# Soft-capped attention with a top-1 expert layer: earlier value loads, ScalarE's releases without GpSimd, a last tile of 32 rows in column tiles

## Chip, cores and metric

One core of a Trainium2 chip runs the whole kernel in one launch. The metric is the device time of one execution in microseconds (us); the median of several executions is compared. Engines are named as in the profile: PE is TensorE (matmul), PEld its weight load, DVE VectorE, ACT ScalarE, POOL GpSimd, SP SyncE.

## What is computed

```python
def _attn_ref(q, k, v, cap):                   # 4 batches, 12 heads, 448 rows, 64 columns
    scores = matmul(q, k.T) / sqrt(64)
    scores = cap * tanh(scores / cap)
    attn = softmax(scores)
    return matmul(attn, v)

def _moe_ref(x, expert_emb, tau, w1, w2):      # x: 1792 x 768, 8 experts, F = 1024
    logits = normed(x) @ normed(expert_emb).T / tau
    e = argmax(logits); gate = softmax(logits)[e]
    out[row] = gate * (relu(x[row] @ w1[e]) @ w2[e])
```

The attention's output, with its heads side by side, is the expert layer's `x`. Each row goes to one expert. With these inputs the experts get 592, 513, 403, 150, 129, 5, 0 and 0 rows, in the order in which the kernel takes them.

## The kernel before

**Attention.** The 48 heads are taken in 24 pairs, two pairs to a unit; a unit has 7 steps. A step makes scores on PE, `tanh` and `exp` on ACT (L860, L864) and, some steps later, the value product on PE (L899), whose rows carry 64 values, 8 columns of the values times the experts' embeddings and a column of ones for the denominator. The embedding columns are made by PE and copied by DVE (L881) into the loaded value rows `vb`. DVE also splits queries and keys into a high and a low part (L828, L829), divides by the denominator and does the routing's counting. `load_heads` (L398 and on) loads keys and queries `qkb`, values `vb` and transposed values `vt` by SP, each into a ring of 2 or 3 buffers. `PARTS` (L74) says at which step of a unit which of the three is loaded, and how many units behind. `odd_heads` (L933) shifts half a batch's columns by a DMA on the same SP queue once DVE has written them, and L463 and L467 write x to a table in DRAM, `x_dram`.

**Expert layer.** All products are in f16 with high and low parts, three matmuls for one. Weights come by SP (`w1r`, `w2r`), and ACT (high part, L250) and DVE (low part, L251) split and scale them for the next expert while PE works on this one. GpSimd fetches 128 rows of x at a time by indirect DMA (`gather`, L221), scales them (`scale_x`, L227), PE turns them round (L238), and ACT and DVE split them into `xh` and `xl` (L241, L242). `tile_body` is a full tile of 128 rows: `up` (L260, 144 matmuls), relu into `hh` and `hl` (L272, L273), and downs (L700) into two PSUM banks, `held`. The output stays there: `release`, at the start of the next tile, scales it on ACT by `held_g` (L311), and GpSimd scatters it to the output rows `held_i` (L312). Up to 32 rows that an expert has beyond its full tiles ride along with one tile of it: `wide_tile` has 160 columns in up (L1475), and the 32 rows' down product is the *along product* (L1518): `hidden` of 32 rows as the stationary side and four column tiles of 32 columns of PE's array, each for a quarter of the 768 output columns. Its output `yo_a` goes through ACT (L1526) and GpSimd (L1527). Here the first expert has five full tiles (the first, hidden under the end of attention, two, and `more0_1`, `more0_2`), the second to fifth have wide tiles (p = 1 to 4) and full ones as needed, and the sixth a half tile (p = 5, 64 columns).

Each tile is inside a branch on a count. At the end of a branch each engine has an exit block (L1607 for the wide tiles, L1646 at the end); GpSimd's waits for all DMAs that it started and then updates their semaphores.

`pace` (FIRST, FIRST0, L86) gives the number of weight splits before each half of up and before each down step. `hooks` run small work at given steps. Instructions go to each engine's queue in program order. The slot of `yo` in `release` comes from two buffers that full tiles share (`tile_of("o")`).

## Time and profile before

| | |
|---|---|
| Time, median of 3 runs (lowest to highest) | 483.21 us (481.74 to 484.41) |
| The profiled execution's own time | 484.38 us |
| Its span in the profile | 482.7 us |
| PE busy | 439.6 us (91%) |
| ACT, DVE, POOL busy | 275.0, 259.9, 126.5 us |
| Mean granted clock of PE | 0.966 |

The span runs from the first instruction to the last, with 1.7 us of the execution outside. Attention and the routing fill it to about 203 us, the expert layer the rest. Times in the text are us from the span's start; in a row of a timeline the number in brackets is how long the engine was idle before the instruction, and what ended that.

### The profile page before, as it was taken

The page shows a single profiled execution, that of the slowest core. Times are in us where ns is not written, and L with a number is a line of the kernel's source. Part 1 is how long each engine was busy: PE and PEld are TensorE (multiplying, and loading weights), DVE is VectorE, ACT ScalarE, POOL GpSimd, SP SyncE. Part 2 cuts the span into 40 slices and gives each one's busy share as a digit, 9 for nine tenths or more (in the row PEclk, how much of TensorE's full clock was granted, in tenths as well). Part 3 has the DMA queues.
Part 4 walks back from the last instruction along what each step waited for, and adds up shares of the span by engine and source line. Part 5 has one row for each costly group of instructions (what it writes and reads, how often), then busy time and mean ns, then how long its engine had stood idle before and what let it go on. Part 6 is the DMA issues. An engine that isn't in the chain of part 4 may idle for free. (4 is left out here: it accounts for less than half of the span.)

```text
span 482.7 us, 16495 instructions
## 1 busy us (share of the span) xinstructions
PE 439.6 (91%) x7001; PEld 352.7 (73%) x7002; DVE 259.9 (54%) x679; ACT 275.0 (57%) x308; POOL 126.5 (26%) x230
## 2 busy tenths in 40 slices
PE   7999998998999699998789989999999999997771
PEld 3788886877878689677477877887887886875561
DVE  5254466558969699884651159211159111964910
ACT  3999998796999786533642067122076122836610
POOL 5000000000010212124362164332155332563720
PEclk9899999898999989999899999999999999998977
DMA  6824559544678652055980269620258521891020
GB/s 194 305 59 143 205 174 336 184 138 177 200 245 255 188 201 88 6 177 186 378 329 3 71 245 406 266 71 1 72 155 309 210 71 19 285 317 56 5 54 27
DMA packets 32457, 82.22 MB, mean 170 GB/s; under 512 B 8253, under 2 KB 13337, under 8 KB 32354
## 3 DMA queue, kind: packets, MB, share of 16 engines
q1 hardware_dynamic: 28754, 67.35, 40.5%
q0 software_dynamic: 2816, 13.49, 8.6%
q8 instruction: 62, 1.02, 0.8%
q14 instruction: 41, 0.34, 0.2%
q10 hardware_dynamic: 784, 0.03, 0.1%
HBM read 68.81 MB, written 12.31 MB: 168 GB/s over the span
## 5 line engine op out<-in xcount | busy, mean ns | idle before, releaser
L899 PEld LDWEIGHTS v<-vb,prob 128*64 128x64 f32 (+1 forms) x2688 | 83.6, 142 | 16.0 <-issue 15.0
L860 ACT ACTIVATE prob<-s,icap 128x896 f32<-128x896 f32 x84 | 80.5, 999 | 18.9 <-PE s L850 15.8
L899 PE MATMUL v<-vb,prob 128*64 128x73 f32 (+1 forms) x2688 | 90.7, 235 | 0.0
L260 PEld LDWEIGHTS <-h 128*128 128x128 f16 x1056 | 79.7, 99 | 5.5 <-issue 3.0
L260 PE MATMUL h<-xh,h 128*128 128x128 f16 (+1 forms) x480 | 78.8, 219 | 3.7 <-DVEq L1607 2.6
L260 PE MATMUL h<-xl,h 128*128 128x128 f16 (+1 forms) x480 | 78.7, 219 | 0.3
L260 PE MATMUL h<-xh,l 128*128 128x128 f16 (+1 forms) x480 | 78.7, 219 | 0.0
L864 ACT ACTIVATE prob<-prob,cap_b 128x1792 f32<-128x1792 f32 (+1 forms) x47 | 76.7, 1632 | 1.5
L251 DVE SCALAR_TENSOR_TENSOR l<-w1r,by_pos,h 128x1024 f16<-128x1024 f32 x30 | 37.1, 1282 | 31.6 <-ACT h L250 31.6
L700 PEld LDWEIGHTS <-hh 128*128 128x128 f16 (+1 forms) x352 | 33.2, 102 | 27.0 <-ACT hh L272 5.7
L260 PEld LDWEIGHTS <-l 128*128 128x128 f16 x528 | 52.1, 99 | 0.5 <-issue 0.5
L700 PE MATMUL v<-h,hh 128*128 128x384 f16 (+1 forms) x176 | 43.0, 338 | 6.3 <-ACT hh L272 5.4
L273 DVE SCALAR_TENSOR_TENSOR hl<-h,hh 128x512 f16<-128x512 f32 (+1 forms) x20 | 13.1, 663 | 65.7 <-ACT hh L272 65.7
L227 POOL TENSOR_TENSOR x_tile<-xg 128x768 f32<-128x768 f32 x16 | 28.4, 1775 | 70.3 <-PE xt L238 65.9
L1475 PE MATMUL h<-xh,h 128*128 128x160 f16 x192 | 39.9, 233 | 3.5 <-PEq L1607 1.4
L700 PE MATMUL v<-l,hh 128*128 128x384 f16 (+1 forms) x176 | 43.0, 337 | 0.0
L700 PE MATMUL v<-h,hl 128*128 128x384 f16 (+1 forms) x176 | 42.6, 335 | 0.0
L251 DVE SCALAR_TENSOR_TENSOR l<-w2r,by_pos,h 128x1536 f16<-128x1536 f32 x20 | 40.4, 2055 | 3.7 <-ACT h L250 3.7
L272 ACT ACTIVATE hh<-h 128x512 f16<-128x512 f32 (+1 forms) x20 | 11.4, 574 | 50.2 <-PE h L260 28.3
L1475 PE MATMUL h<-xh,l 128*128 128x160 f16 x192 | 39.9, 233 | 0.0
L1475 PE MATMUL h<-xl,h 128*128 128x160 f16 x192 | 39.9, 233 | 0.0
L241 ACT CAST xh<-xt 128x384 f16<-128x384 f32 x30 | 12.8, 478 | 45.2 <-PE xt L238 45.2
(287 smaller groups left out, 797.1 us busy)
## 6 DMA issues: line engine op xcount, KB each, us to landing
w1r<-in_moe_w_dram SPq DMA_DIRECT2D x30, 512.0 KB, 9.1
w2r<-in_moe_w_dram SPq DMA_DIRECT2D x20, 768.0 KB, 7.0
qkb<-in_qk_pairs_dram SPq DMA_DIRECT2D x11, 896.0 KB, 6.8
vb<-in_v_pairs_dram SPq DMA_DIRECT2D x12, 511.0 KB, 5.2
vt<-in_vt_pairs_dram SPq DMA_DIRECT2D x12, 448.0 KB, 7.1
x_dram<-xsb SPq DMA_DIRECT2D x12, 432.0 KB, 3.9
ring<-in_moe_w_dram SPq DMA_DIRECT2D x6, 512.0 KB, 5.6
ring<-in_moe_w_dram SPq DMA_DIRECT2D x5, 384.0 KB, 4.5
```

The lines of the kernel that those rows point to most:

```text
L227: nc.gpsimd.tensor_tensor(x_tile.rearrange("p (h d) -> p h d", d=DH), heads(xg[:, :SCALE]), xg[:, SCALE : SCALE + 1].unsqueeze(2).to_broad ...
L241: nc.scalar.copy(hi, t)
L251: nc.vector.scalar_tensor_tensor(out=lo, in0=raw, scalar=scale, in1=hi, op0=ALU.mult, op1=ALU.subtract, accum_out=acc)
L260: nc.tensor.matmul(hp[:, f, :W], l[j][:, c], x[:, j, :W], start=j == 0 and f == 0 and n == 0, stop=j == DC - 1 and f == 3 and n == 2, skip ...
L272: nc.scalar.activation(b, a, AF.Relu)
L273: nc.vector.scalar_tensor_tensor(out=c, in0=a, scalar=0.0, in1=b, op0=ALU.max, op1=ALU.subtract, accum_out=acc[:, h : h + 1])
L700: nc.tensor.matmul(y, hidden[h][l][:, c, :W], w2p[p % 2][w][f // 2][:, f % 2, m * C : (m + 1) * C], start=f == 0 and n == 0, stop=f == FC ...
L860: nc.scalar.activation(o, sp[:, :, :S], AF.Tanh, scale=icap)
L864: nc.scalar.activation(o, o, AF.Exp, scale=cap_b)
L899: nc.tensor.matmul(psum_v[2 * i + n][h * DH : (h + 1) * DH, m * VW : (m + 1) * VW], pt[rows, s, c : c + DH], vb[rows, k, s, :], start=m == ...
L1475: nc.tensor.matmul(o, w1p[p % 2][l][j][:, c], x[:, j, :], start=j == 0 and f == fs[0] and m == 0, stop=j == DC - 1 and f == fs[-1] and m == 2,
```

## The change

1. The value rows are loaded in the sixth step of a unit instead of in the second of the next, the transposed values and the keys a step or several earlier (`PARTS`).
2. The order of small work around the first tiles: `token_rows` of the last batch moves from before the first tile's downs to the second tile's start; the routing's last pieces move into the ups; `FIRST0` puts one weight split instead of three and two before the first two halves of chain 0's first tile; the along rows' transposes use PSUM banks of their own.
3. `gate` and `held_g` are computed by ACT instead of GpSimd. Releases in wide tiles and in the last tile write to `rows[p % 2]`, two slots of their own in `room`.
4. In `wide_tile` the along product stands before the transposes of the next x, and its output in ACT's and GpSimd's queues with it; the last wide tile leaves `scale_x` and `gather` to the branch for further tiles.
5. The sixth and later experts' last rows, now up to 32 instead of 64, go through `small_tile`: x is the stationary side (32 columns), the weights move through four column tiles, then the hidden layer is turned round by two transposes.

```diff
-PARTS = {5: ("k", 0), 0: ("t", 1), 2: ("v", 1)}
+PARTS = {2: ("t", 0), 4: ("k", 0), 6: ("v", 0)}
-FIRST, FIRST0 = (4, 4, 1), (3, 2, 1)
+FIRST, FIRST0 = (4, 4, 1), (1, 1, 1)
 ...
-    def hold(idx, unscaled):
-        nc.gpsimd.tensor_tensor(held_g, gate, unscaled, op=ALU.mult)
+    def hold_rows(idx):
         nc.gpsimd.tensor_copy(held_i, idx)
-    def release():
-        yo = tile_of("o", 0)
+    def hold_gates(unscaled):
+        nc.scalar.activation(held_g, gate, AF.Copy, scale=unscaled)
+    def release(yo=None):
+        yo = tile_of("o", 0) if yo is None else yo
 ...
     def wide_tile(...)
-        release()
+        release(rows[p % 2])
 ...
+        hold_gates(unscaled)
+        hold_rows(col(base))
 ...
-        transpose_x()
-        scale_x()
-        ya = tile_of("h", 0)
+        ya = tile_of("s", 0)
         for f in range(FC):
             ...
-        down(6)
-        down(7)
         nc.scalar.activation(yo, ya[:, :C], AF.Copy, scale=ga)
         nc.gpsimd.indirect_dma_start(out=..., in_=yo, ...)
-        gather(col(base + 3))
+        transpose_x()
+        if p + 1 < WIDE.stop:
+            scale_x()
+        down(6)
+        down(7)
+        if p + 1 < WIDE.stop:
+            gather(col(base + 3))
 ...
+    def small_tile(p, before=()):
+        ...
+        for m in range(BLOCKS):
+            nc.scalar.activation(
+                gt[m * TAIL : (m + 1) * TAIL], gate[:TAIL], AF.Copy, scale=by_pos[:TAIL, 2, p : p + 1]
+            )
+        for j in range(DC):
+            for k, (x, w) in enumerate(((xh, 0), (xl, 0), (xh, 1))):
+                for m in range(BLOCKS):
+                    nc.tensor.matmul(
+                        hp[m * TAIL : (m + 1) * TAIL], x[:, j, :TAIL], w1p[p % 2][w][j][:, m * n : (m + 1) * n], ...
+                    )
+        nc.scalar.copy(h32, hp)
+        for c in range(2):
+            nc.tensor.transpose(t[:, c * P : (c + 1) * P], h32[:, c * P : (c + 1) * P], ident)
+        relu(0, t[:, : 2 * P].rearrange("p (c t) -> p c t", t=P), acc, (hh, hl))
+        for f in range(FC):
+            for k, (l, w) in enumerate(passes):
+                for m in range(BLOCKS):
+                    nc.tensor.matmul(
+                        y[m * TAIL : (m + 1) * TAIL], (hh, hl)[l][:, f % 2, b],
+                        w2p[p % 2][w][f // 2][:, f % 2, m * C : (m + 1) * C], ...
+                    )
+        nc.vector.tensor_scalar(yo, y, gt, None, op0=ALU.mult)
+        nc.gpsimd.indirect_dma_start(out=..., in_=yo, ...)
 ...
-            half_tile(p, {0: [lambda: foretell("more", ends[p][0] > 1), release]}, fine_sums)
+            small_tile(p, [lambda: release(rows[p % 2])])
+            foretell("more", ends[p][0] > 1)
+            fine_sums()
             overflow(False)
```

**SP in attention.** `vb` are value rows, `qkb` keys and queries, `vt` transposed values; the copies of `xsb` on itself are `odd_heads`. Before, around the first late load of value rows:

```order
28 L933 DMA xsb_201<-xsb_201 64x2x72
29 L463 DMA x_dram<-xsb_201 384x1x288
30 L403 DMA qkb_207<-in_qk_pairs_dram 128x2x896
31 L467 DMA x_dram<-xsb_201 64x864
32 L403 DMA vt_212<-in_vt_pairs_dram 128x896
33 L933 DMA xsb_202<-xsb_202 64x2x72
34 L463 DMA x_dram<-xsb_202 384x1x288
35 L403 DMA vb_210<-in_v_pairs_dram 128x1022
```

With the change, from the same `odd_heads` copy on:

```order
29 L908 DMA xsb_198<-xsb_198 64x2x72
30 L464 DMA x_dram<-xsb_198 384x1x288
31 L404 DMA qkb_204<-in_qk_pairs_dram 128x2x896
32 L404 DMA vb_207<-in_v_pairs_dram 128x1022
33 L468 DMA x_dram<-xsb_198 64x864
34 L908 DMA xsb_199<-xsb_199 64x2x72
```

The value rows of the unit (`vb_210` before, `vb_207` now) moved from behind the second `odd_heads` copy to right behind the unit's `qkb`.

**ACT at the end of the last wide tile** (`w2r` are raw weights, `yo_a` the along product's output, `held_g` the output's scale). Before:

```order
381 L250 ACTIVATE h_4836<-w2r_4850,by_pos 128x1536
382 L250 ACTIVATE h_4837<-w2r_4851,by_pos 128x1536
383 L250 ACTIVATE h_4838<-w2r_4852,by_pos 128x1536
384 L241 CAST xh<-xt_8439 128x3x128
385 L241 CAST xh<-xt_8445 128x3x128
386 L1526 ACTIVATE yo_a<-h_8454,gta 128x192
387 L1607 COMPARE_AND_BRANCH
```

With the change:

```order
410 L249 ACTIVATE h_4825<-w2r_4839,by_pos 128x1536
411 L249 ACTIVATE h_4826<-w2r_4840,by_pos 128x1536
412 L249 ACTIVATE h_4827<-w2r_4841,by_pos 128x1536
413 L1489 ACTIVATE yo_a<-s_8444,gta 128x192
414 L240 CAST xh<-xt_8546 128x3x128
415 L240 CAST xh<-xt_8552 128x3x128
416 L242 COPY gates_179<-gates_179 128x1
417 L1630 COMPARE_AND_BRANCH
```

`yo_a` moved from behind both halves of `xh` to before them, and a gate copy that was GpSimd's follows them.

**POOL at the same place.** `xg` is the gathered x, `x_tile` the scaled one. Before:

```order
505 L243 COPY gates_182<-gates_182 128x1
506 L227 TENSOR_TENSOR x_tile<-xg 128x768
507 L231 COPY gates_182<-xg 128x1
508 L1527 DMA out_dram<-yo_a,idx_a 7168x192
509 L220 ISA
510 L220 COPY idx_in<-table 128x1
511 L221 DMA xg<-x_dram,idx_in 128x866
512 L1607 COMPARE_AND_BRANCH
```

With the change (`room` now holds the released rows):

```order
474 L303 COPY held_i<-table 128x1
475 L1490 DMA out_dram<-yo_a,idx_a 7168x192
476 L1630 COMPARE_AND_BRANCH
477 L226 TENSOR_TENSOR x_tile<-xg 128x768
478 L230 COPY gates_179<-xg 128x1
479 L219 ISA
480 L219 COPY idx_in<-table 128x1
481 L220 DMA xg<-x_dram,idx_in 128x866
```

The two gate copies L243 and the scaling, L227, stood before the write of `yo_a`; now the write comes first and the branch L1630 right behind it, and scaling and gather stand in that branch's body, which is not taken here.

## Rows read from the trace of the kernel before

**Rows 1.** Busy time by stretch; core 0: us, then each engine's busy us, clock, DMA.

```profile
40.00:60.00 20.00, 20.00 (x428) 16.10 (x428) 9.20 (x18) 19.50 (x17) 0.25 (x2) 1.00 0.46 151
84.00:88.00 4.00, 3.50 (x44) 2.78 (x44) 2.69 (x7) 2.13 (x2) 1.13 (x2) 0.57 0.39 156
```

**Rows 2.** Table of waits: us in total, times, longest.

```profile
DVE vb L881 <- DMA vb<-in_v_pairs_dram: 15.9, 4, 4.1
```

**Rows 3.** Timeline of SyncE's queue: start, us, engine, line, what.

```profile
59.72 0.57 SPq L403 DMA_DIRECT2D qkb<-in_qk_pairs_dram  x1
...
70.76 0.62 SPq L933 DMA_DIRECT2D xsb<-xsb  x1
...
72.13 0.56 SPq L403 DMA_DIRECT2D vb<-in_v_pairs_dram  x1
```

**Rows 4.** The tile vb, all its loads.

```profile
DMA to landing us min/median/max: 4.9/5.2/7.2
```

**Rows 5.** Timeline of ScalarE behind three stalls; in brackets its idle time before.

```profile
85.83 1.01 ACT L860 ACTIVATE prob<-s,icap 128x896 f32<-128x896 f32 x1 [2.77 <-PE s L850]
...
89.64 1.91 ACT L860 ACTIVATE prob<-s,icap 128x896 f32<-128x896 f32 x2 [0.98 <-PE s L850]
...
111.28 1.91 ACT L860 ACTIVATE prob<-s,icap 128x896 f32<-128x896 f32 x2 [2.48 <-PE s L850]
...
116.56 1.91 ACT L860 ACTIVATE prob<-s,icap 128x896 f32<-128x896 f32 x2 [1.55 <-PE s L856]
...
169.91 1.97 ACT L860 ACTIVATE prob<-s,icap 128x896 f32<-128x896 f32 x2 [3.71 <-PE s L850]
...
174.98 1.91 ACT L860 ACTIVATE prob<-s,icap 128x896 f32<-128x896 f32 x2 [1.27 <-PE s L856]
```

**Rows 6.** Timeline of TensorE, ScalarE and VectorE in chain 0's first tile.

```profile
234.87 0.82 PE L700 MATMUL v<-h,hh 128*128 128x384 f16 x2 [2.82 <-ACT hh L272]
...
242.98 1.57 ACT L250 ACTIVATE h<-w2r,by_pos 128x1536 f16<-128x1536 f32 x1 [2.11 <-DMA w2r<-in_moe_w_dram]
...
246.34 1.02 DVE L242 TENSOR_TENSOR xl<-xt,xh 128x384 f16<-128x384 f32 x2
...
247.04 0.92 PE L1423 MATMUL along_t<-ident,room 128*128 128x128 f32 x6 [1.80 <-DVE xl L242]
```

**Rows 7.** Timeline of TensorE: first matmuls of the last tiles, and a gap.

```profile
408.23 0.23 PE L1475 MATMUL h<-xh,h 128*128 128x160 f16 x1 [0.74 <-PEq L1607]
...
426.88 0.50 PE L1501 MATMUL v<-h,hh 128*128 128x384 f16 x2
...
429.82 0.23 PE L1475 MATMUL h<-xh,h 128*128 128x160 f16 x1 [0.82 <-DVEq L1607]
...
458.91 0.19 PE L260 MATMUL h<-xh,h 128*128 128x64 f16 x1 [2.61 <-DVEq L1607]
...
467.37 0.53 PE L700 MATMUL v<-h,hh 128*64 128x384 f16 x2 [2.56 <-ACT hh L272]
```

**Rows 8.** Timeline of ScalarE and VectorE, fifth expert and half tile.

```profile
438.39 1.05 ACT L311 ACTIVATE yo<-v,held_g 128x384 f32<-128x384 f32 x2 [10.90 <-DMA out_dram<-yo,held_i]
...
466.94 0.66 ACT L272 ACTIVATE hh<-h 128x256 f16<-128x256 f32 x2
...
467.35 0.42 DVE L273 SCALAR_TENSOR_TENSOR hl<-h,hh 128x256 f16<-128x256 f32 x1 [8.65 <-ACT hh L272]
```

**Rows 9.** Instructions of line 1607, the ends of the tile branches, 427 to 445 us.

```profile
L1607 POOLq INC_SWDGE_SEM  x1: 806/806/806, 437.5 to 437.5; - x1
```

**Rows 10.** Timeline of GpSimd, fifth expert and last write.

```profile
440.24 1.02 POOL L312 DMA_INDIRECT out_dram<-yo,held_i  x1 [8.78 <-ACT yo L311]
443.54 0.72 POOL L1447 TENSOR_TENSOR gta<-along_g,by_pos 32x1 f32<-32x1 f32 x1 [2.27 <-issue]
...
448.51 0.41 POOL L1453 COPY gta<-gta 32x1 f32<-32x1 f32 x2
...
473.89 0.98 POOL L742 DMA_INDIRECT out_dram<-yo,idx_out  x1 [4.12 <-DVE redo_i L1571]
```

**Rows 11.** Busy time of line 1518, the along product, in one wide tile.

```profile
298.60:300.90 2.30, 2.17 (x96) 1.94 (x96) 1.00 1.01 388
```

**Rows 12.** The tile yo_a, its four writes.

```profile
DMA to landing us min/median/max: 5.5/6.3/6.5
```

More of the change, by code (lines that the diff above doesn't have):

```diff
@@ L144, in attention_moe @@
         nc.gpsimd.memset(round_up[:, n, :], float(P - 1 - (1 - n) * TAIL))
-    blocks_of = {}
-    for n in (2, 4):
-        blocks_of[n] = const.tile([P, 1], I32, name=f"block{n}")
-        for m in range(n):
-            nc.gpsimd.memset(blocks_of[n][m * P // n : (m + 1) * P // n], m)
+    BLOCKS = P // TAIL
+    block = const.tile([P, 1], I32, name="block")
+    for m in range(BLOCKS):
+        nc.gpsimd.memset(block[m * TAIL : (m + 1) * TAIL], m)
     tok = const.tile([P, B, 4], F32, name="tok")
@@ L242, in transpose_x @@
             nc.vector.tensor_tensor(lo, t, hi, op=ALU.subtract)
-        nc.gpsimd.tensor_copy(gate, gate_s)
+        nc.scalar.copy(gate, gate_s)
     def split(raw, hi, lo, scale, acc, vector=False):
@@ L654, in tiles, with tile_body @@
             nc.vector.tensor_tensor(done_full, done, full[:, 0, :], op=ALU.add)
-        def tile_body(p, idx, nxt, W=P, todo=(), pace=FIRST, hooks=(), hidden=None, first=False, before=None, holds=True):
+        def tile_body(p, idx, nxt, todo=(), pace=FIRST, hooks=(), hidden=None, first=False, holds=True):
             hooks, todo = dict(hooks), list(todo)
@@ L663, in tile_body @@
             if holds:
-                yb = [t[:, :384] for t in held]
                 if not first:
@@ L700, in down @@
                         nc.tensor.matmul(
-                            y, hidden[h][l][:, c, :W], w2p[p % 2][w][f // 2][:, f % 2, m * C : (m + 1) * C],
-                            start=f == 0 and n == 0, stop=f == FC - 1 and n == 2, skip_group_check=W < P,
-                        )
-            if first:
-                hold(idx, unscaled)
+                            y, hidden[h][l][:, c, :], w2p[p % 2][w][f // 2][:, f % 2, m * 384 : (m + 1) * 384],
+                            start=f == 0 and n == 0, stop=f == FC - 1 and n == 2,
+                        )
             if not hidden:
@@ L714, in tile_body @@
                         hook(h * DC + j)
-                        if holds and (h, j) == (1, 1):
-                            hold(idx, unscaled)
-                        up(w1p[p % 2], h, j, hp[h], W)
-                    hidden.append(relu(h, hp[h], acc, W))
+                        up(w1p[p % 2], h, j, hp[h])
+                    hidden.append(relu(h, hp[h], acc))
                 nc.vector.tensor_tensor(sum_h[:, :2], sum_h[:, :2], acc, op=ALU.add)
+            if holds:
+                hold_gates(unscaled)
+                hold_rows(idx)
             for f in range(6):
@@ L1058, in attention_bounded @@
                 ready = {
-                    0: [do_fill, do_fill], 3: square[:1], 5: [*square[1:], lambda: norms_x(last)],
+                    0: [lambda: [f() for _, _, f in route], do_fill, do_fill], 3: square[:1], 5: [*square[1:], lambda: norms_x(last)],
                     7: [count_last, do_fill], 8: [do_fill],
@@ L1069, in attention_bounded @@
                     do_fill()
-                for _, _, f in route:
-                    f()
-                token_rows(last)
                 tile_body(0, idx0[:, 0:1], None, hidden=first_h, first=True)
@@ L1353, in attention_moe @@
         0: [
-            lambda: scales_x(last), lambda: gates(last), lambda: gates_e(last), order, start_loads,
+            lambda: token_rows(last), lambda: scales_x(last), lambda: gates(last), lambda: gates_e(last), order, start_loads,
             lambda: gates_out(last), slots,
@@ L1546, in col @@
         return table[:, bass.ds(t, 1)]
-    def any_tile(p, slot, nxt, *args, **kw):
-        tile_body(p, col(slot), nxt is not False and col(nxt), *args, **kw)
     def full_tile(p, slot, *args, **kw):
-        any_tile(p, slot, slot + 3, P, *args, holds=p < WIDE.stop, **kw)
+        tile_body(p, col(slot), col(slot + 3), *args, holds=p < WIDE.stop, **kw)
+    rows = [room[:, n * D : (n + 1) * D] for n in range(2)]
     fine = work.tile([P, NF], F32, tag="fine", name="fine")
@@ L1590, in todo_for @@
             return [(split1, p, i) for i in range(SOON if p == 1 else 0, N1)] + [(split2, p, f) for f in range(N2)]
-        def half_tile(p, hooks=(), before=None):
-            any_tile(p, ends[p][1], False, P // 2, hooks=hooks, before=before, holds=False)
         def chain(p):
@@ L1660, in attention_moe @@
                 load2(LATE, f, True)
+            with tc.If(ends[WIDE.stop - 1][0] >> 1 == 1):
+                scale_x()
+                gather(col(ends[WIDE.stop][1] + 2))
             position(WIDE.stop)
```

119 lines of the change are left out of this document (65 added, 54 removed).

## Prediction

> **What bounds the kernel now.** I read the busy time by stretch first. In an undisturbed stretch of attention TensorE is busy 20.00 of 20.00 us at a granted clock of 1.00 and ScalarE 19.50 [rows 1]: both are full, so time lost there by either is not made up. In the stretch 84 to 88 us the clock is 0.57, the lower of its two levels (1.2 GHz) for most of it [rows 1], and it follows an empty TensorE. So I looked next, in the table of waits and the timelines, for what empties TensorE. Three places stand out: VectorE waits for the value rows `vb` in attention (15.9 us in four times) [rows 2]; the first expert tile waits for its hidden layer [rows 6]; and the end of the kernel, where ScalarE stands 10.90 us before the fifth expert's release and TensorE then waits 2.61 and 2.56 us [rows 7, 8]. What TensorE does elsewhere the change leaves alone.
>
> **A, attention: the loads.** SyncE issues the key load at 59.72 but the value rows only at 72.13, behind the odd-heads copy that waits for VectorE [rows 3]; they land about 5.2 us later [rows 4], and VectorE's copy L881 stands in front of all its other work until then. The change issues the value rows right behind the key load of the same unit, some 12 us earlier, so they lie there before the copy comes to them. On SyncE the writes of x and the weight loads go behind one more issue of 0.56 to 0.57 us [rows 3]; they are read many us later, which hides it. The stalls' worth I take from ScalarE, which was full: its idle gaps behind three of the four are 2.77 + 0.98, 2.48 + 1.55 and 3.71 + 1.27, together 12.76 us [rows 5] (the second gap of each pair is TensorE at the lower clock). The fourth left no such gap and counts nothing. 12.76 is a ceiling, since ScalarE has half a us of idle in 20 anyway [rows 1]: I take **-12.0**. Bounds: -13.5, if the lower clock cost a little beyond ScalarE's gaps, and -3, if only one stall goes and VectorE's own work is late next in the other two.
>
> **B, the first tiles.** The hidden layer of chain 0's first tile stands behind weight splits on ScalarE that wait for DMA; TensorE waits 2.82 us for it [rows 6]. With one split before each half instead of three and two, it no longer does. But the last `w2r` split waits for its load until 242.98 whatever comes before, VectorE's `xl` stands behind that split's second half until 246.34, and TensorE waits for `xl` [rows 6]. So most of the 2.82 us is a wait moved, not removed: Up of the next tile can start when the first `xl` half is there, near 246.9, while before it came behind the along rows' transposes, 0.92 us from 247.04 [rows 6]; these now have PSUM tiles of their own and go ahead of it. I take **-0.9**. The token rows, moved from before the first tile into the next one's start, and the gates' write, moved earlier, touch waits on VectorE and SyncE in front of a TensorE gap that ScalarE ends; nothing for them. Bounds 0 (the load stays the bound) and -2.8 (the whole gap goes).
>
> **C, wide tiles.** The along product (2.17 us, [rows 11]) goes before the transposes of the next x. `xh` and `xl` then have only two down steps as cover instead of these and the product, as in a full tile. On ScalarE the product's output `yo_a` now stands before `xh`; on GpSimd its write stands before the scaling of x and the gather, which come some 2 us later and are needed a tile later. I take **0**, between -1 and +3.6 (twice the 1.80 us that TensorE waits for `xl` where it is late, [rows 6]).
>
> **D, into the fifth expert's wide tile.** ScalarE's release at 438.39 had waited 10.90 us [rows 8]: it needs `held_g` from GpSimd, and GpSimd was in its exit block, whose semaphore update came at 437.5 and took 0.8, once the tile's gather and writes had landed [rows 9]. All weight splits, the hidden layer and VectorE's tail stand behind it, and so the half tile starts at 458.91 [rows 7]. After the change `held_g` and the gate are ScalarE's own, and the release writes into a slot that was read two tiles ago. ScalarE then starts with TensorE, as in the tile before, which took 429.82 - 408.23 = 21.59 us with its exit [rows 7]. The small tile would start at 429.82 + 21.59 = 451.4 instead of 458.91: -7.5. Next in line is `yo_a`, which needs `gta` from GpSimd: GpSimd still sits in its exit block to 438.3, and its chain ended at 448.9 [rows 10]. The product would end about 447.6: 451.4 less 2.94, from the first matmul behind the product, 426.88, to the next tile's [rows 7], and less 0.9 for six transposes [rows 6]. So `yo_a` waits about 1.3 us and `xh`, `xl` come at 450.2 and 450.8: still in time, with 0.6 us to spare.
>
> **E, the small tile and the end.** Up becomes 18 groups of four matmuls of 256 columns, each in a quarter of the array. The same form at 192 columns took 2.17 us for 24 groups, 90 ns each [rows 11]; by columns 120 ns, 18 x 0.12 = 2.2 us instead of 5.9 (458.91 to 464.8). Then a copy, two transposes, relu and the low half: by the evictions of 128x256 (0.33 each on ScalarE, 0.42 on VectorE, [rows 8]) and about 0.8 for the transposes and hand-overs, 1.9 us of TensorE idle instead of 2.56. Downs: 24 groups of 192 columns, 2.2 us as in rows 11 (up to 4.3 if the clock is at its lower level). Output scaling 0.4. TensorE's side is ready at 451.4 + 2.2 + 1.9 + 2.2 + 0.4 = 458.1.
>
> GpSimd's side: `yo_a` is written from 449.4; it has no gather beside it any more. Its landing took 5.5 to 6.5 us under load [rows 12]; the release's took 3.3 (440.24 to 443.54, [rows 10]) on a quiet chip. Between 3.0 and 5.5 I take 4.0, nearer the quiet row because the chip is quiet here: 453.4. Exit block 0.8 [rows 9] and branches 0.5: release issued 454.7. The final write waits for that release's landing, 3.3 on: 458.0, and 0.3 of branch and semaphore. So both sides are ready near 458 to 459, and I take 459.0 against 473.89 [rows 10]: **-14.9** for D and E, between -16 and -11.5 (landings of 5.5, and the lower clock for down). The time from this issue to the span's end, 482.7 - 473.89 = 8.8 [rows 10], stays: the sums and the test for overflow, now behind the output, take 1.7 us beside its landing.
> By the Trainium skill ("DMA: Bandwidth & Descriptors", "Anatomy of one DMA — SWDGE (gpsimd) path") a write costs about 2.0 us fixed plus its bytes at 436 GB/s: an estimate of 2.2 and 2.9 us for the two landings in place of 4.0 and 3.3. By that rule GpSimd's side would be ready 2.2 us earlier, TensorE's 458.1 would rule, and D and E would give -15.8. The rows at hand (3.3 and 5.5) lie above the rule's figures, so the sum keeps them.
>
> **Sum.** -12.0 - 0.9 + 0 - 14.9 = -27.8. On the profiled run's 484.4 that is 456.6. That run is 1.2 above the median of the runs shown, 483.2: I forecast **455.4** for a median.
>
> **Rivals.**
> 1. *The loads help little* (A fails): a load can't start before its slot in the ring is free, and VectorE may be late by itself. Against it: the slots are of three units ago, and the key loads at the same point of the queue do go out [rows 3]. Only one stall gone, -3: 464.4. This holds also the case that the edit doesn't do what it says.
> 2. *GpSimd's chain rules the end*: two landings of 5.5 instead of 4.0 and 3.3, or a longer exit: final write 2 to 4 us later, about 458.5. For it: the earlier landings of `yo_a` [rows 12].
> 3. *Slower*: `yo_a` stands before `xh` on ScalarE and waits for GpSimd's index chain, which waits for a landing. If the chain ended late in each of the four wide tiles, `xh`, `xl` and the next tile would all wait. It decides from where the chain ends over 1.9 us after the product (1.3 is forecast for the worst tile, with 0.6 to spare). To eat the gain it must end 7 us past that point in all four: at 8 us each, 32 - 27.8 = 4 us slower, 487. Against it: the chain ran to 448.9 in the latest tile [rows 10], 19 us into it.
> 4. *Gap of the first tile and its clock go fully*, and the wide tiles' waits with them: 3 us more, 452.4.
>
> **Chances.** Forecast 0.60 (its own range 452.5 to 457.5), first rival 0.12, second 0.15, third 0.01, fourth 0.10, other 0.02. For 8 in 10 the range goes down past the fourth (450, with A's -13.5 on top) and up past the second to most of the first: **450 to 463**. A measurement of this kernel can tell about 0.5%, 2.4 us, from no change. Faster by more: 0.97, same 0.02, slower 0.01.
>
> **What would show it.** Right: VectorE has no wait for `vb` at L881 and ScalarE no 2 to 4 us gaps in attention; the release into the fifth expert starts within 1 us of TensorE's first matmul; the small tile's up takes near 2.2 us; `xl` or the last `w2r` load still ends a wait before the second tile of chain 0; the last GpSimd write goes out near 446 on the new span (459.0 less the 12.9 of A and B), the span about 455. Wrong: ScalarE gaps of the old size in attention, a TensorE wait for `xh` or `xl` after a wide tile, four column tiles that run one after another (up over 4 us), or an end over 9 us behind the last write.

## The result, and the profile after

The changed kernel took **464.91 us** (median of 4 runs, 464.17 to 465.32), the kernel before beside it 482.95: a ratio of 0.9624 (95% interval 0.9593 to 0.9654). It is faster, as forecast, but by 18.0 us between the medians (19.7 between the profiled runs) and not by 27.8, and 464.91 lies above the range of 450 to 463. The profiled runs took 484.38 and 464.71, -19.67, with 1.7 us outside the span in both; the spans, 482.7 and 463.0, can be set against each other stage by stage. On the page PE went from 439.6 to 428.1 busy us (92%), ACT from 275.0 to 280.6, POOL from 126.5 to 108.6, the granted clock from 0.966 to 0.979.

The table has the starts of stages (first matmul of up, from the timelines of TensorE) and what each part gained (-) or lost (+):

| stage begins | before | after | change of the part before it | forecast |
|---|---|---|---|---|
| end of the first tile's downs | 202.58 | 191.41 | -11.17 (A) | -12.0 |
| chain 0's second full tile | 203.66 | 193.33 | +0.84, branch exit | 0 |
| third full tile | 223.84 | 215.18 | +1.67, the second tile | 0 |
| `more0_1` | 247.79 | 237.51 | -1.62, the third tile | -0.9 (B) |
| `more0_2` | 264.29 | 256.69 | +2.68, `more0_1` | 0 |
| wide tile p = 1 | 282.17 | 274.46 | -0.11 | 0 |
| wide tile p = 4 | 429.82 | 421.34 | -0.77 (C) | 0 |
| last tile | 458.91 | 444.01 | -6.42 (D) | -7.5 |
| last GpSimd write | 473.89 | 454.07 | -4.92 (E) | -7.4 |
| end of span | 482.7 | 463.0 | +0.1 | 0 |

The third tile is the one that the prediction calls chain 0's first (its wait for `hh` is in [rows 6]), and `more0_1` is that one's next tile.

**Attention.** The table of waits after (us in total, times, longest) has only this for the value rows' copy on VectorE, L856 now, where [rows 2] showed 15.9 us for a DMA:

```profile
DVE vb L856 <- PE ve L852: 12.6, 9, 2.7
```

ScalarE's six gaps of [rows 5] are gone. Between the first unit and the routing two gaps over 1 us are left, and both follow a TensorE stop in which nothing in the profile is awaited ("issue"). Timelines of TensorE and ScalarE:

```profile
68.37 1.36 PE L874 MATMUL v<-vb,prob 128*64 128x73 f32 x35 [1.23 <-issue]
...
108.24 0.47 PE L874 MATMUL v<-vb,prob 128*64 128x73 f32 x7 [1.33 <-issue]
...
70.80 1.91 ACT L835 ACTIVATE prob<-s,icap 128x896 f32<-128x896 f32 x2 [1.60 <-PE s L825]
...
109.90 1.91 ACT L835 ACTIVATE prob<-s,icap 128x896 f32<-128x896 f32 x2 [1.56 <-PE s L831]
```

**The first expert's tiles.** TensorE (timeline) now stands 1.92 us before the second tile, where it stood 1.08, and 4.34 us behind the third, for the scaled along rows; the windows behind both gaps have the clock at 0.76 and 0.66, the one between at 1.00:

```profile
193.33 0.22 PE L259 MATMUL h<-xh,h 128*128 128x128 f16 x1 [1.92 <-DVEq L1173]
...
236.18 0.90 PE L1394 MATMUL s<-ident,room 128*128 128x128 f32 x3 [4.34 <-POOL room L1383]
```

```profile
193.00:200.00 7.00, 6.67 (x91) 6.70 (x92) 5.94 (x38) 1.47 (x4) 1.29 (x2) 0.76 0.39 119
226.00:234.00 8.00, 5.84 (x38) 3.61 (x36) 6.11 (x8) 4.67 (x3) 1.32 (x2) 1.00 1.03 412
234.00:244.00 10.00, 7.38 (x75) 7.15 (x76) 4.87 (x7) 4.67 (x9) 8.16 (x14) 0.66 0.74 273
```

Behind the second gap the matmuls of up stand 0.107 us apart instead of 0.056: the lower of the two levels. GpSimd's timeline says why the along rows are late: its copy into `held_i` waits until the release of 226.60 has landed beside weight loads (the DMA share of 226 to 234 is 1.03), and the scaling stands behind it.

```profile
226.60 1.03 POOL L312 DMA_INDIRECT out_dram<-yo,held_i  x1 [0.30 <-issue]
234.52 0.18 POOL L303 COPY held_i<-table 128x1 int32 x1 [6.89 <-DMA out_dram<-yo,held_i]
234.67 1.46 POOL L1383 TENSOR_TENSOR room<-room 128x768 f32<-128x768 f32 x1
```

**The fifth expert's wide tile.** The 10.90 us of [rows 8] are gone: ScalarE's release starts at 421.10, before TensorE's 421.34. But `yo_a` waits 4.03 us, and `xh` behind it. Timeline of ScalarE:

```profile
421.10 1.05 ACT L311 ACTIVATE room<-v,held_g 128x384 f32<-128x384 f32 x2 [1.47 <-PEq L1630]
...
442.01 0.42 ACT L1489 ACTIVATE yo_a<-s,gta 128x192 f32<-128x192 f32 x1 [4.03 <-POOL gta L1420]
442.33 0.85 ACT L240 CAST xh<-xt 128x384 f16<-128x384 f32 x2
```

and of GpSimd from there to its last write, against [rows 10]:

```profile
434.31 1.17 POOL L1417 TENSOR_TENSOR gta<-along_g,by_pos 32x1 f32<-32x1 f32 x1 [2.29 <-issue]
435.43 5.49 POOL L1506 COPY idx_a<-along_i 32x1 int32<-32x1 int32 x4
...
441.56 0.41 POOL L1420 COPY gta<-gta 32x1 f32<-32x1 f32 x2
...
442.84 1.06 POOL L1490 DMA_INDIRECT out_dram<-yo_a,idx_a  x1 [0.59 <-ACT xh L240]
448.35 0.97 POOL L312 DMA_INDIRECT out_dram<-room,held_i  x1 [4.46 <-ACT hh L270]
454.07 0.97 POOL L1559 DMA_INDIRECT out_dram<-room,small_i  x1 [4.75 <-ACTq L1685]
```

The four copies of 32 x 1 numbers took 5.49 us. In the kernel before the same four took 1.84 (its timeline):

```profile
444.20 1.84 POOL L1449 COPY idx_a<-along_i 32x1 int32<-32x1 int32 x4
```

The chain of waits of the changed kernel cuts the copies apart (start, us), and VectorE's timeline shows what ran beside them:

```profile
435.48 1.74 POOL idx_a L1506
437.26 1.70 POOL idx_a L1506
439.00 1.70 POOL idx_a L1506
440.74 0.19 POOL idx_a L1506
```

```profile
435.36 1.82 DVE L250 SCALAR_TENSOR_TENSOR l<-w2r,by_pos,h 128x1536 f16<-128x1536 f32 x1
...
437.10 1.82 DVE L250 SCALAR_TENSOR_TENSOR l<-w2r,by_pos,h 128x1536 f16<-128x1536 f32 x1
...
438.83 1.82 DVE L250 SCALAR_TENSOR_TENSOR l<-w2r,by_pos,h 128x1536 f16<-128x1536 f32 x1
```

Each of the first three copies ends within 0.05 us of the end of one weight split (437.18, 438.92 and 440.65), and the last, when VectorE has none left, takes 0.19. The whole chain from `gta` to its last copy grew by less than the four copies, from 5.4 to 7.7 us: in the kernel before, two other small instructions of it (L1450, L1451) took 1.16 and 1.09 us beside `w1r` splits, and the same two take 0.22 and 0.19 now. The Trainium skill ("SBUF — State Buffer", "SBUF: two separate sides") says that a VectorE instruction with two inputs in SBUF and a GpSimd instruction that reads SBUF lock each other out for a whole instruction; these rows agree with it.

**The small tile.** TensorE, and the two landings as the chain of waits has them:

```profile
444.01 0.29 PE L1533 MATMUL h<-h,xh 128*32 128x256 f16 x4 [1.86 <-DVEq L1630]
444.12 0.29 PE L1533 MATMUL h<-h,xl 128*32 128x256 f16 x4
```

```profile
442.84 2.92 DMA out_dram<-yo_a,idx_a
...
446.00 0.79 another core or an unknown queue
...
448.35 4.86 DMA out_dram<-room,held_i
```

Four column tiles do run side by side, a group of four every 0.11 us. VectorE scales the output at 450.73 for 0.42 us, so TensorE's side is ready at 451.15. GpSimd's last write starts 2.9 us later, 0.86 behind the landing of the release (448.35 + 4.86 = 453.21).

### The profile page after: what moved, and what is told of

It is laid out like the page before. It is cut to its first block, busy times and chain, and to the rows that moved or that the text cites. A ratio compares the mean times of both kernels' runs of the same rounds, so it can differ in the third digit from the quotient of the medians.

```text
span 463.0 us, 16449 instructions
## 1 busy us (share of the span) xinstructions
PE 428.1 (92%) x6979; PEld 346.1 (75%) x6980; DVE 256.3 (55%) x677; ACT 280.6 (61%) x341; POOL 108.6 (23%) x195
## 3 DMA queue, kind: packets, MB, share of 16 engines
q8 instruction: 63, 1.03, 0.9%
## 5 line engine op out<-in xcount | busy, mean ns | idle before, releaser
L874 PEld LDWEIGHTS v<-vb,prob 128*64 128x64 f32 (+1 forms) x2688 | 78.8, 136 | 18.2 <-issue 16.8
L259 PE MATMUL h<-xh,h 128*128 128x128 f16 x432 | 76.4, 224 | 1.9 <-DVEq L1173 1.9
L259 PE MATMUL h<-xl,h 128*128 128x128 f16 x432 | 76.3, 224 | 0.4 <-DVE xl L241 0.4
L259 PE MATMUL h<-xh,l 128*128 128x128 f16 x432 | 76.3, 224 | 0.0
L684 PEld LDWEIGHTS <-hh 128*128 128x128 f16 x320 | 30.8, 98 | 19.8 <-issue 1.8
L684 PE MATMUL v<-h,hh 128*128 128x384 f16 x160 | 39.1, 326 | 1.3 <-ACT h L249 1.2
L250 DVE SCALAR_TENSOR_TENSOR l<-w2r,by_pos,h 128x1536 f16<-128x1536 f32 x20 | 35.8, 1825 | 7.2 <-ACT h L249 7.1
L684 PE MATMUL v<-h,hl 128*128 128x384 f16 x160 | 39.1, 326 | 0.0
L684 PE MATMUL v<-l,hh 128*128 128x384 f16 x160 | 39.1, 326 | 0.0
L226 POOL TENSOR_TENSOR x_tile<-xg 128x768 f32<-128x768 f32 x15 | 22.6, 1509 | 68.8 <-PE xt L237 52.8
```

The costliest lines, as they stand in the source:

```text
L226: nc.gpsimd.tensor_tensor(x_tile.rearrange("p (h d) -> p h d", d=DH), heads(xg[:, :SCALE]), xg[:, SCALE : SCALE + 1].unsqueeze(2).to_broad ...
L250: nc.vector.scalar_tensor_tensor(out=lo, in0=raw, scalar=scale, in1=hi, op0=ALU.mult, op1=ALU.subtract, accum_out=acc)
L259: nc.tensor.matmul(hp[:, f, :], l[j][:, c], x[:, j, :P], start=j == 0 and f == 0 and n == 0, stop=j == DC - 1 and f == 3 and n == 2, skip_ ...
L684: nc.tensor.matmul(y, hidden[h][l][:, c, :], w2p[p % 2][w][f // 2][:, f % 2, m * 384 : (m + 1) * 384], start=f == 0 and n == 0, stop=f == ...
L874: nc.tensor.matmul(psum_v[2 * i + n][h * DH : (h + 1) * DH, m * VW : (m + 1) * VW], pt[rows, s, c : c + DH], vb[rows, k, s, :], start=m == ...
```

## The experiments

All edits are to the changed kernel. Single runs of one kernel lie up to 7 us apart (455.92 to 463.10 in experiment 5), so where there is only one it is read by its stages, and these too come from one profile; where three or more runs were taken the median and the lowest and highest stand beside the time.

**1. The index chain ahead of the release.** In `wide_tile` the release and the `w2` loads move behind the piece that computes `gta` and `idx_a`, so that GpSimd does it before VectorE's `w2r` splits.

```diff
-        release(rows[p % 2])
-        for f in range(N2): load2(p + 1, f)
         ... (gta and idx_a)
+        release(rows[p % 2])
+        for f in range(N2): load2(p + 1, f)
```

> One edit to the changed kernel: in each wide tile GpSimd builds the along rows' index and gate (gta) before the release's write is issued, not behind it. Theory: in the last wide tile the along product's output waits 4.03 us on ScalarE for gta, because GpSimd issues the release first, waits for its landing and then runs its copies beside VectorE's splits; xh, xl, the small tile's start and the chain of two landings at the end hang on it. Then the wait falls under 1 us, the small tile starts about 1 us earlier after the fifth expert's start (near 21.6 us instead of 22.67), the last GpSimd write goes out 2 to 4 us earlier and the whole is 461 to 463 us instead of 464.9. Rival: GpSimd stands in its exit block until about 9 us into the tile anyway and the copies are slow, so gta stays late: 464.9, within 0.5 us.

Measured: 462.62 us (461.25 to 463.83). GpSimd:

```profile
432.37 0.85 POOL L1506 COPY idx_a<-along_i 32x1 int32<-32x1 int32 x4
...
452.78 0.97 POOL L1559 DMA_INDIRECT out_dram<-room,small_i  x1 [3.84 <-DVE fine_s L1592]
```

The copies take 0.85, the wide tile 21.97 instead of 22.67, and from the small tile's start to the last write it is 8.20 instead of 10.06: `yo_a` and the exit are earlier, and now the output scaled by VectorE (ready at 451.93, 0.85 before the write; the profile names a VectorE instruction behind it) comes last. The chain was a cause of both D's and E's shortfall.

**2. The token rows back before the first tile's downs' end.** One call moves back to its old places.

```diff
+                token_rows(last)
 ...
-            lambda: token_rows(last), lambda: scales_x(last), ...
+            lambda: scales_x(last), ...
```

> One edit to the changed kernel: the last batch's token rows are computed before the first tile's downs again, as in the kernel before. Theory: the 1.92 us that TensorE waits between the first tile and the next at 191.4 is VectorE's exit from the branch, which nothing hides once the token rows (0.98 us of VectorE) have gone from before it; the lower clock from 194 to 198 follows from that gap. Then the gap is near 1.1 us, the clock in the 5 us behind it 1.00, and the second tile's first up to the third tile's first up takes 20.2 us instead of 21.85; the whole is 463 to 463.7. Rival: the exit takes its 2.4 us whatever stands before it; then the gap is 1.9 to 2.9 us, the lower clock stays, and the whole is 464.9 or up to 1 us more.

Measured: 462.45 (462.20 to 463.48). The gap before the second tile is 0.93, and the same window as above has the clock at 1.00:

```profile
193.44 0.23 PE L259 MATMUL h<-xh,h 128*128 128x128 f16 x1 [0.93 <-ACTq L1175]
```

```profile
193.00:200.00 7.00, 6.56 (x118) 6.56 (x119) 5.95 (x36) 1.88 (x4) 1.28 (x2) 1.00 0.39 115
```

The second tile takes 20.23 us as before (20.18), not 21.85. VectorE's timelines show the gap's cause. In the changed kernel:

```profile
193.41 0.16 DVE L1607 TENSOR_TENSOR sums<-sums,acc 128x2 f32<-128x2 f32 x1 [2.48 <-DVEq L1173]
```

and with the token rows (L547) back:

```profile
191.02 0.98 DVE L547 TENSOR_SCALAR a_all<-iota_p,rowf,tok 128x128 f16<-128x128 f16 x4
...
193.15 0.16 DVE L1609 TENSOR_TENSOR sums<-sums,acc 128x2 f32<-128x2 f32 x1 [0.23 <-DVEq L1175]
```

VectorE comes out of the branch 2.48 us behind its last work without the token rows in front and 0.23 behind it with them. The two profiles can't be set against each other by their starts alone: in this one the whole stretch lies 1.1 us later, from before the token rows on (TensorE's downs end at 192.5 instead of 191.4). But over all profiles with the new loads the second tile starts at 192.28 to 194.92 with the token rows behind the exit (ten) and at 193.25 to 193.84 with them in front (four). So the work taken out before the exit saved nothing that shows; TensorE only stood longer.

**3. The old numbers of splits before the first halves.**

```diff
-FIRST, FIRST0 = (4, 4, 1), (1, 1, 1)
+FIRST, FIRST0 = (4, 4, 1), (3, 2, 1)
```

> One edit to the changed kernel: three, two and one weight splits are put ahead of the halves of the first expert's third tile again, instead of one each. Theory: the smaller number moved TensorE's wait to the end of that tile (4.34 us before the along rows' transposes) and saved 1.6 us from the tile's first up to the next one's, but the lower clock that follows the longer gap costs about 2.5 us in the next tile, where before it fell into this one. Then this kernel shows a wait of 2 to 3 us for hh in the third tile again, 23.5 to 24 us for it instead of 22.3, and 33.2 to 34.4 us instead of 36.95 for the two tiles behind it: the whole is the same or up to 1 us faster, 464 to 465. Rival: the edit is a plain gain of 1.6 us; then this kernel is 466.5.

Measured: 461.60 (459.59 to 464.53). TensorE:

```profile
192.98 0.22 PE L259 MATMUL h<-xh,h 128*128 128x128 f16 x1 [1.88 <-DVEq L1173]
...
224.47 0.82 PE L684 MATMUL v<-h,hh 128*128 128x384 f16 x2 [3.06 <-ACT hh L270]
```

The old wait for `hh` is back (3.06, in [rows 6] 2.82), but it stands in place of the 4.34 us for the along rows, not on top of it. Third tile and `more0_1` together take 40.05 us; over all runs with three and two splits it is 40.0 to 40.3 (four runs), with one and one 40.7 to 41.6. So this edit of the change costs about 1 us. The expectation had this trade, but not its sizes: the third tile took 22.24 us and not 23.5 to 24, and the whole came out under 464, because the second tile, too, was faster in this profile. Against what experiment 2 suggests, its clock stayed at 1.00 behind a gap of 1.88, and it took 20.22:

```profile
193.00:200.00 7.00, 7.00 (x126) 7.00 (x127) 6.23 (x40) 1.00 (x3) 1.29 (x2) 1.00 0.44 133
```

**4. The gap filled.** Nine matmuls of 512 columns, whose result nothing reads, end the first tile's downs.

```diff
+                z = ps_s.tile([P, 2, 4, P], F32, tag="s", ...)[:, 0]...
+                for _ in range(9):
+                    nc.tensor.matmul(z, w1p[0][0][0][:, :P], w1p[0][0][0][:, P : P + 512], start=True, stop=True)
```

> One edit to the changed kernel: nine matmuls of 512 columns (1.9 us at the full clock) into a bank that nobody reads, behind the first tile's downs, so that TensorE is not idle while the branch is left at 191.4; it adds work and takes none away. Theory: the lower clock from 194 to 198 comes from the idle 1.92 us; with the gap filled the clock stays 1.00 and the second tile's first up to the third's takes 20.2 us instead of 21.85, so the whole is 463.0 to 463.5 though work was added. Rival: the clock falls for another reason (the load of the up itself); then the whole is 464.9 or, if the added matmuls hold up the exit, 1 to 2 us more.

Measured: 462.71 (462.18 to 466.11).

```profile
191.54 2.11 PE L1048 MATMUL cover<-h 128*128 128x512 f16 x9
193.95 0.22 PE L259 MATMUL h<-xh,h 128*128 128x128 f16 x1 [0.30 <-PEq L1176]
```

The second tile takes 20.22: with TensorE kept busy the clock stays up, though the gap's own time is spent. One profile shows little by itself, since the clock also stayed up behind four of ten unfilled gaps of about 2 us (last section).

**5. Edits 1, 2 and 3 together.**

> The three edits of tok_back, first0_back and gta_first together on the changed kernel. If each acts on its own place, as their traces showed (second tile 20.2 us for 21.85, third and fourth together 40.05 for 41.5, fifth expert to the last GpSimd write 30.2 for 32.7), they add up: 1.6 + 1.5 + 2.1 = 5.2 us less than the changed kernel, 459.5 to 460.5 us. Rival: the clock's stretches only move to the next gap; then 462 to 463.

Measured: 459.59 (455.92 to 463.10), ratio to the kernel before 0.9427 (0.9355 to 0.9498).

**6. The gate and `held_g` back on GpSimd**, the rest of the change left.

```diff
-        nc.scalar.copy(gate, gate_s)
+        nc.gpsimd.tensor_copy(gate, gate_s)
-        nc.scalar.activation(held_g, gate, AF.Copy, scale=unscaled)
+        nc.gpsimd.tensor_tensor(held_g, gate, unscaled, op=ALU.mult)
```

> One edit to the changed kernel: held_g and the gate are computed by GpSimd again, the release's slots stay. Theory: either dependence on GpSimd is enough to hold ScalarE's release at the fifth expert's start until GpSimd has left its exit block, 9 us into the tile; then the release waits 8 to 10 us, the small tile starts 27 to 29 us after that start instead of 22.67, and the whole is 469 to 471. Rival: only the slots mattered (the wait was named for a DMA); then the release starts within 1 us and the time is 464.9.

**7. The releases back into the shared buffers.**

```diff
-        release(rows[p % 2])
+        release()
```

> One edit to the changed kernel: the releases of the wide tiles and of the small tile write into the two shared buffers again, held_g stays on ScalarE. Theory: these buffers' semaphores need GpSimd's exit block too, so the release waits 8 to 10 us at the fifth expert's start, the small tile starts 27 to 29 us after it, and the whole is 469 to 471. Rival: only held_g mattered; then the release starts within 1 us and the time is 464.9.

Measured (one run each): 466.33 and 469.72. ScalarE's release into the fifth expert, with 6 and with 7:

```profile
425.93 1.05 ACT L311 ACTIVATE room<-v,held_g 128x384 f32<-128x384 f32 x2 [5.44 <-POOLq L1630]
```

```profile
429.07 1.05 ACT L311 ACTIVATE yo<-v,held_g 128x384 f32<-128x384 f32 x2 [10.11 <-DMA out_dram<-yo,held_i]
```

The wide tile takes 24.44 and 28.29 us instead of 22.67. Each wait alone comes back, GpSimd's exit with 5.44 (8 to 10 were expected) and the buffer's landing with 10.11; [rows 8] showed the later of the two. The prediction put the 10.90 on `held_g` and GpSimd's exit; the slots carry the larger part, and both edits are needed.

**8. The loads as before**: `PARTS = {5: ("k", 0), 0: ("t", 1), 2: ("v", 1)}`.

> One edit to the changed kernel: PARTS as in the kernel before, so the value rows go out late again; everything else as changed. Theory: the loads' share is the whole of what came ahead of the expert layer, so VectorE waits about 4 us for vb four times, TensorE's gaps of 1.9 to 3.7 us and the lower clock behind three of them come back, and the second tile's first up moves from 192.98 to 194.9 (the runs so far) to 203 to 205, 10 to 11 us later; the whole is 474 to 476 us. Rival: other parts of the change (the routing's order) carry a share of it; then the start is 200 to 202.

Measured (one run): 472.24. The table of waits has the value rows again, and the second tile starts at 203.47, as in the kernel before (203.66); with the new loads that start lay between 192.28 and 194.92 in all other runs. So the loads carry all of A, within what single runs scatter. The whole is some 2 us under the expected 474 to 476; the second tile's clock stayed up here (20.22 us), which is 1.6 of it.

```profile
DVE vb L856 <- DMA vb<-in_v_pairs_dram: 22.5, 5, 5.8
```

**9. The value rows in the first step of the next unit** (`0: ("v", 1)` for `6: ("v", 0)`), for the "issue" gaps.

> One edit to the changed kernel: the value rows of a unit are loaded one step pair later than in the change (first step of the next unit), no longer right behind the keys, and still ahead of the second odd-heads copy. Theory: TensorE's waits of 0.6 to 1.3 us at 68 to 70 and at 108 to 110 us, which no engine ends, come from its instructions arriving behind two loads in a row; with the loads apart they fall under 0.5 us and VectorE still doesn't wait for vb; the second tile's first up is at 191 to 192.5. Rival: they belong to that place in the program; then they stay, and the start is 193 to 195. A third outcome: the later load makes VectorE wait for vb again, by up to 4 us at a time; then the start is later than 195.

Measured (one run): 465.38. L856 waits for no DMA, the gap near 68 us is gone, that near 108 stays (1.66), and the second tile starts at 193.73, no earlier (191 to 192.5 were expected). Experiment 4 has no gap near 68 either. What those gaps are stays open. A variant that loads the value rows at the same unit's first step computed something else: its branches ran further tiles (18058 instructions instead of 16449), and its 600.20 us say nothing of the loads.

**10. TensorE made later**, by nine idle matmuls of 512 columns (2.1 us) before the small tile's up.

> One edit to the changed kernel: nine matmuls of 512 columns (1.9 us) into an unused bank ahead of the small tile's up; work is added and nothing taken away. Theory: the last write waits for GpSimd's side (landing of yo_a, exit, release, its landing), which is ready 3.0 us after TensorE's; then the last GpSimd write goes out as long after the fifth expert's start as without them (32.7 us, within 0.4), and the span does not grow. Rival: TensorE's side sets the end; then both grow by 1.9 us.

Measured (one run): 463.22. The last write comes 31.34 us after the start of p = 4 instead of 32.73 (32.7 within 0.4 was expected): 2.1 us of work on TensorE cost nothing, so its side had room in the changed kernel and GpSimd's ruled. Here TensorE's output is the last (ready at 451.03, write at 451.80). The release's landing is not in this profile; issued at 447.50, it can have taken at most 3.5 us, where the changed kernel's took 4.86.

**11. The best version so far with the next expert's `w1` loads later**, to let the last `w2r` load in.

```diff
-        load1(p + 1, i)
+        if p != 1: load1(p + 1, i)
 ... (the six loads called behind the along rows' transposes)
```

> The three edits of combo_all, and the loads of the third expert's first weights go out at the end of the first expert's third tile instead of behind each split in it. Theory: in that tile all of TensorE's waiting (3.1 us for hh, 0.6 to 1.2 us for xl behind it, and the lower clock in between) comes from the second expert's weights, which share 400 GB/s with these six loads of 512 KB; without them the last w2r load lands 5 to 7 us earlier, the tile takes 17 to 18.5 us from its first up to the next one's instead of 22.2 to 23.0, and the whole is 455 to 457 us. Rival: the loads are set by something else (their queue, the number in flight), and the tile stays at 22 us; then 459.6.

Measured: 459.20 (458.25 to 461.73), not 455 to 457. It failed in its purpose: SyncE, which runs ahead of the other engines, still issued them at 222.19,

```profile
222.19 5.57 SPq L1202 DMA_DIRECT2D w1r<-in_moe_w_dram  x6
```

the last `w2r` split still came at 233.18, and third tile plus `more0_1` took 40.07, as without it.

**12. `yo_a` behind `xh` on ScalarE** (`transpose_x()` moved ahead of the along product's output, the product left where it is).

> One edit to the changed kernel: in a wide tile the along product's output goes through ScalarE behind the two halves of xh, not ahead of them; TensorE's order is untouched. Theory: the 1.1 us by which the small tile starts late after the fifth expert's start (22.67 us for 21.59) is xh standing on ScalarE behind yo_a, which waits for gta; then the small tile starts 21.6 to 22.0 us after it, but yo_a's write still goes out when gta is there (21.5 us after the start), the end hangs on that, and the whole is the same as the changed kernel within 1 us. Rival: the exit of the branch alone makes it late; then it stays at 22.67.

Measured (one run): 462.50. `xh` starts without the index chain, the wide tile takes 21.92 instead of 22.67 and the small tile 8.64 up to the last write. So the order on ScalarE is what let the late chain reach TensorE: experiment 1 mends the chain, this one the order, with the same 0.7 us. The whole was to stay within 1 us of the changed kernel and came out 2.4 under it: in this profile the release landed after 3.2 us, not 4.86, and the second tile kept its clock (20.22).

**13. Changed kernel and experiment 5 again, on one chip.**

> The changed kernel itself, once more, on the same chip as combo_again, to see its spread and to compare the two: 463 to 466 us. In the trace, a gap of about 1.9 us ahead of the second tile, and 20.2 us for that tile if the clock holds, 21.85 if it falls.

> The kernel of combo_all (token rows back in front, three and two splits again, index and gate ahead of the release) on the same chip as after_again: 458 to 461 us, 3 to 6 us under after_again. Rival: combo_all's spread (455.9 to 463.1) was luck and the two are within 1.5 us.

Measured: 463.98 (461.53 to 466.56) and 460.08 (457.80 to 462.26), 6 runs each; ratios to the kernel before 0.9585 (0.9533 to 0.9636) and 0.9498 (0.9447 to 0.9549). Experiment 5 is 3.9 us faster by the medians, beside 5.3 the first time. It gains less than 1, 2 and 3 apart (2.3, 2.5 and 3.3 below 464.91), in part, by the profiles, since 2 and 3 share one gain: the second tile is at 20.2 in each of them. And it loses a part at the end, where the small tile up to the last write takes 10.23 us, against 8.20 in experiment 1. TensorE there, and in experiment 12 at the same place:

```profile
440.09 0.29 PE L1535 MATMUL h<-h,xh 128*32 128x256 f16 x4 [1.10 <-ACT room L311]
...
441.69 0.40 PE L1535 MATMUL h<-h,xh 128*32 128x256 f16 x3 [1.01 <-issue]
...
442.53 0.63 PE L1535 MATMUL h<-l,xh 128*32 128x256 f16 x4
442.75 0.63 PE L1535 MATMUL h<-h,xh 128*32 128x256 f16 x4
```

```profile
442.63 0.29 PE L1533 MATMUL h<-h,xh 128*32 128x256 f16 x4 [1.10 <-ACTq L1630]
...
444.23 0.29 PE L1533 MATMUL h<-h,xh 128*32 128x256 f16 x3 [1.01 <-issue]
...
444.80 0.38 PE L1533 MATMUL h<-h,xh 128*32 128x256 f16 x4
444.91 0.38 PE L1533 MATMUL h<-h,xl 128*32 128x256 f16 x4
```

Behind the same two gaps the groups stand 0.21 us apart in the one and 0.11 in the other.

## Why the prediction was wrong, step by step

The direction was right, and so were the mechanism of A, the release's of D and the four column tiles of E; the sum was 8.1 us too good (the median 9.5: the 1.2 us taken off for a median did not come either, since the profiled run of the changed kernel was no slower than its median). By the table the 8.1 are 0.8 in A, 4.4 in B with the tiles around it, -0.8 in C, 1.1 in D, 2.5 in E and 0.1 in the tail.

- **A, right.** -11.2 for -12.0. Experiment 8 gives 8.6 to 11.2 back (203.47 less the starts of the other runs). The first rival, that the loads help little, is out: no wait of VectorE for the loads is left.
- **B, "nothing for them", failed.** The prediction hid the token rows behind "a TensorE gap that ScalarE ends" and did not ask who ends it once ScalarE is early. Now it is VectorE's branch exit, 2.48 us behind VectorE's last work: 1.92 instead of 1.08, and then the lower clock, +0.84 and +1.67 us. Experiment 2 takes back both; that the gap is what drops the clock rests on all profiles together (last section), not on this one alone. What holds VectorE in the exit for so long without work is not shown.
- **B, "-0.9", was too small for the third tile and missed the next.** That tile gained 1.62, since its `hh` gap went with the lower clock behind it (0.67 in the kernel before, in the row below), while the wait at its end grew from 1.80 to 4.34. The forecast let `more0_1` start as soon as `xl` was there, near 246.9 of the old time; in fact TensorE stood 4.34 us for the along rows, which wait on GpSimd for a release's landing of 7.9 us, a chain that the prediction left out. Behind that gap `more0_1` ran partly at the lower clock, +2.68. Experiment 3 shows that the old splits are better by about 1 us over both tiles.

```profile
234.80:240.00 5.20, 5.13 (x21) 2.40 (x22) 4.63 (x7) 4.35 (x5) 1.64 (x3) 0.67 1.04 407
```

- **C, right, and 0.77 better by luck.** -0.77 for 0, within its bounds; no full tile behind a wide one stands for `xh` or `xl`. The gain lies in places that the prediction did not price: two full tiles behind wide ones took 16.50 us instead of 16.80 each.
- **D, "still in time, with 0.6 us to spare", failed.** The forecast let the index chain end where it had ended before, 19.1 us into the tile (448.92 against 429.82). It ended at 441.97, 20.6 us into it, 1.5 later: it started 0.75 earlier in the tile and took 2.3 longer, since its copies, moved against VectorE's schedule, met the `w2r` splits of 1.74 us and not those of `w1r`. The third rival had this mechanism and its point of decision right, at a worth of 0.7 us in one tile and not in all four: it named 1.9 us behind the product, the chain ended 2.57 behind it (product to 439.40), 0.67 past that point, and experiments 1 and 12 take 0.7 back each; what is left there over the forecast's 21.59, 0.3 to 0.4, is about the longer exit gap (1.10 to 1.16 in them, 0.82 in [rows 7]).
- **E, "3.3 on", was mis-sized, and the second rival, that GpSimd's chain rules the end, was right.** From the small tile's start to the last write the forecast was 459.0 - 451.4 = 7.6; it took 10.06. TensorE's side came in 7.1 us (6.7 forecast), so it was not this. GpSimd's side, from `yo_a`'s write on: landing 2.92 for 4.0, from there to the release's issue 2.59 (0.79 of it the semaphore update) for 1.3, landing 4.86 for 3.3, and 0.86 for 0.3. It also started only 1.2 us before TensorE, not 2.0, since the index chain held it. Experiment 10 shows that this side ruled. How much of it is scatter the other profiles tell: with the fifth expert and the end left alone (the changed kernel again, 2, 3, 4, 8, 9) this stretch took 8.58 to 10.54, the release's landing 3.7 to 5.2 where the profile has it, so 7.6 was too short in all of them. The 3.3 itself was read too long: from 440.24 to 443.54 is up to GpSimd's next instruction, and the profile has 3.1 for that landing. The estimate by the Trainium skill ("DMA: Bandwidth & Descriptors", "Anatomy of one DMA — SWDGE (gpsimd) path") of 2.2 and 2.9 us is too low for the release's 4.86 and for `yo_a`'s 2.92; only the shortest landings of all profiles, 2.3 and 3.0, come down to it.
- **The range.** Its upper end let the loads fail alone; no case let several small waits fall due at once, and none priced a gap's clock outside the first tile's `hh`.

## What to carry to other kernels

When work is taken from in front of a wait that another engine ends, ask which engine ends it next: here VectorE's branch exit and GpSimd's landing took the places of ScalarE's split. A handful of tiny GpSimd instructions is costed by the VectorE instructions it will stand beside (1.7 us a copy beside a long split, 0.2 alone), so place them where VectorE works short or not at all. And a chain that ends a program in two indirect writes is to be priced by the longest landing seen, each exit and hand-over included.

## What the runs showed of the hardware

- **A gap of about 2 us drops TensorE's clock in some executions and not in others.** Before the second tile the gap was 1.88 to 2.20 us in ten profiled runs. The tile behind it took 21.80 to 21.85 us in six of them (the changed kernel's two, experiments 1, 6, 9 and 10; gaps 1.92 to 2.20) and 20.2 in four (3, 7, 8 and 12; gaps 1.88 to 2.18). With gaps of 1.18 or less it took 20.2 in all six (the kernel before, 2, 4, 5, 5 again in 13, and 11). What decides between 1.88 and 2.20 is open; the fall costs 1.6 us there. The last tile shows the same: behind two gaps of 1.10 and 1.01 us the clock fell in experiment 5 run again and stayed up in experiment 12, and in experiment 5's first profile it fell behind 1.17 and 0.81.
- **One small GpSimd copy per VectorE split**: 1.70 to 1.74 us each beside `w2r` splits of the changed kernel, 0.19 alone.
- **Landings of a release of 128 rows**: 3.0 to 5.2 us in the last tile of twelve profiles of the changed kernel and its edits (4.86 in the first), 3.1 in the kernel before, 7.9 beside weight loads. The along rows' write of the fifth expert took 2.3 to 4.3 in eleven.
